# A planner's rules replaced by an order written out by hand, and banks open to all: relu-squared attention and a gated feed-forward layer on one core

## The chip, the cores and the metric

The kernel runs on one NeuronCore of a Trainium2 chip. The metric is device time in microseconds of one execution; the kernel before has a median of 409.42 us over 3 runs. One further execution was recorded by the hardware profiler, and all profile lines come from it.

## The reference

```python
# q, k, v: (8 batches, 12 heads, 448 positions, 64)
scores = (1 / sqrt(64)) * q @ k.transpose
attn   = maximum(scores, 0) ** 2 / 448
x      = (attn @ v), heads side by side           # (3584 tokens, 768)
gate   = maximum(x @ w_gate, 0)                   # w_gate, w_val: 768 x 1536
out    = (gate * (x @ w_val)) @ w_out             # w_out: 1536 x 768, out float32
```

There is no softmax, so a score tile needs only a relu and a square before it is multiplied with V.

## The kernel before

**Engines.** TensorE (PE) does all products and some transposes. VectorE (DVE) and ScalarE (ACT) empty its accumulation banks and do the elementwise work. GpSimd (POOL) issues the loads, SyncE (SP) the transposing transfers and the stores.

**Attention** goes in groups of four heads ("quads"), three to a batch, 24 in all; batch 0 is done in two parts of 192 and 256 query columns, so the list of attention objects `A_` has 27 entries. A group's queries and keys are loaded to `raw`, transposed to `qkT` (for batches 0 and 1 by TensorE, lines L535, L542 and L582; from batch 2 on a copy `perm` on DVE, L606, and then two transposing transfers by SP). `s(step)` (L681) makes one slot of scores: four matmuls on 64x64 tiles of the array, side by side, into a pair of neighbouring banks. Its relu (L692 on ACT or L694 on DVE) and its square (L704 or L706) leave `at`. When all 7 slots of a group are there, `pv()` (L723) multiplies them with V: 28 matmuls on 64x64 tiles into another pair of banks, copied to `xT` (L738 or L740).

**Feed-forward** works on 128x128 tiles. Batches 0 and 1 take plain products (`gv_plain`, L787). The later batches go in pairs through one level of Strassen's method: `gv_strassen` makes seven products (L896) for each of 12 blocks of the hidden width, in three banks, where later products are added to earlier ones after those have been copied out (`snapshot`, L843/L847); `out_both` does the same for the output weights (L1013). So a chain of products keeps a bank for a while.

**Banks.** There are eight. A score slot or a `pv` takes a pair, chosen from PAIRS, MORE_PAIRS or FIRST_PAIRS; a product takes a single one from SINGLES:

```python
    PAIRS, MORE_PAIRS, FIRST_PAIRS = [0, 2], [0, 2, 4], [0, 2, 4, 6]
    SINGLES = [7, 6, 5, 4]
```

**Order.** The program is written as operations (`Op`) with their engines, prices, needed operations and buffers. `plan` walks through planned time: at each step it takes the operation that could start first by the prices, and the emitted program on every engine is the list of operations sorted by planned start. Each engine then runs its own list in that order and waits where an operand or a bank is not ready. Prices are written as (time until the engine is free, time until the result is there), for instance `A448, V448 = (0.455, 0.6), (0.533, 0.66)` for a copy of 448 columns on ACT and DVE. Before, `plan` chooses TensorE's next operation between the head of the attention list (`att`) and a window of the feed-forward list (`ffn`) by a debt account: RESERVE, WINDOW, START, LATEST, HOLD, SLACK, CUTS, SPARE and APART are its settings. The loads form one list for POOL (`pool_ops`), in the order of `Planner.ORDER`; `load_gv` brings two blocks of the gate and value weights, `load_out` a quarter of the output weights. Until 21 us of planned time a `filler` of dummy matmuls (L1169) is put into gaps of TensorE's order.

Of the kernel before, what the change touches and what calls it, by code (L numbers as in the profile page):

```python
# [41 lines left out]
class Op:  # L42


    def __init__(self, engs, emit, deps=(), alloc=(), reads=(), mode=None, grp=None):
        self.engs, self.emit = engs, emit
        self.deps, self.alloc, self.reads = list(deps), list(alloc), list(reads)
        self.mode, self.grp = mode, grp
        self.load = self.land = 0.0
        self.kind = None  # L50
        self.cut = self.edge = False
        self.xbar = 0
        self.start = self.end = self.eng = None
        for b in self.reads:
            b.readers += 1


class Planner:
# [5 lines left out]
    RESERVE = (1000.0, 4.0, 3.0)  # L64
# [4 lines left out]
    WINDOW = (5, 5)  # L69
    ATT_WINDOW = (3, 1)  # L70
    START = (0.7, 0.8)
    LATEST = (1.8, 3.0)
    HOLD = (0.1, 0.05)
    SLACK = (0.2, 0.1)
    CUTS = ((1, 3), (1, 5, 6), (2, 4, 6), (2, 6))
# [7 lines left out]
    SCORES_FIRST = 0.0  # L83
# [4 lines left out]
    SPARE = -0.3  # L88
    APART = (0.5, 0.5)
# [84 lines left out]
def plan(first, att, ffn, others, pool, goals, filler, banks):  # L174

    P = Planner(banks)  # L180
    ai = pi = 0
# [6 lines left out]

    def done(op):
        for o in outs.get(id(op), ()):  # L190
            o.missing -= 1
            if not o.missing:
                active.append(o)

    att, ffn = list(att), list(ffn)
    last_grp = None
    inside, debt, share = False, 0.0, 0.0
    left_work = {}
    for o, sg in ffn:
        left_work[sg] = left_work.get(sg, 0.0) + o.engs["PE"][0]  # L200

    def set_share():
        sg = ffn[0][1] if ffn else None
        left = goals[sg] - ai if sg is not None and goals[sg] is not None else 0
        work = left_work[sg] - P.RESERVE[min(sg, 2)] if left > 0 else 0.0
        return max(0.0, work) / max(1, left)

    def fits(ops, now, late):

        among, width = ops[0].alloc[0].among, ops[0].alloc[0].width  # L210
        times = sorted(max(P.free_at(i + w) for w in range(width)) for i in among)
        for o, t in zip(ops, times):
            if t > now + P.SLACK[late]:
                return False
            now += o.engs["PE"][0]
        return True

    first = [list(x) for x in first]
    while any(first) or att or ffn or active or pi < len(pool):
        cands = []  # L220
        late = int(not ffn or ffn[0][1] >= 3)
        for op in active:
            b = P.best(op)
            if b is not None:
                cands.append((b[0] + P.YIELD.get(op.kind, 0.0), b[2] - P.URGENT.get(op.kind, 0.0), 1, b[1], op, b[0]))
        if pi < len(pool):
            b = P.best(pool[pi])
            if b is not None:
                s = b[0]
                if pi >= P.NOUT:  # L230
                    s = max(s, P.landed[pi - P.NOUT])
                cands.append((s, 0.0, 0, "POOL", pool[pi]))
        pick = None
        if any(first):
            for i, x in enumerate(first):
                b = P.best(x[0]) if x else None
                if b is not None:
                    cands.append((b[0] + (P.SCORES_FIRST if i == 0 else 0.0), b[2], 3, "PE", x[0], b[0]))
            b = P.best(att[0]) if P.SPARE is not None and att else None
            if b is not None:  # L240
                s = b[0] + att[0].engs["PE"][0] + P.SPARE
                if all(c[2] != 3 or s <= c[0] for c in cands):
                    cands.append((b[0], b[2], 4, "PE", att[0]))
        else:
            A = F = None
            for i, op in enumerate(att[:P.ATT_WINDOW[late]]):
                b = P.best(op)
                if b is not None and (A is None or b[0] < A[0] - 0.03):
                    A = (*b, i)
            for i, (op, _) in enumerate(ffn[:P.WINDOW[late]]):  # L250
                b = P.best(op)
                if b is not None and (F is None or b[0] < F[0] - 0.03):
                    F = (*b, i)
            if last_grp is not None and ffn and last_grp == ffn[0][0].grp:
                b = P.best(ffn[0][0])
                F = (*b, 0) if b is not None else None
                pick = "F" if F is not None else None
                if F is not None and A is not None and A[0] + att[A[3]].engs["PE"][0] + P.APART[late] <= F[0]:
                    pick = "A"
            elif A is not None and F is not None:  # L260
                now = P.t.get("PE", 0.0)
                if inside:
                    pick = "A" if A[0] <= max(F[0], now + P.HOLD[late]) else "F"
                else:
                    n = next((i for i, o in enumerate(att) if o.cut), len(att) - 1) + 1
                    if debt >= P.LATEST[late] * n * share:
                        pick = "A" if A[0] <= F[0] + 0.15 else "F"
                    elif debt >= P.START[late] * n * share and A[0] <= now + 0.15 and (ffn[0][0].edge or ffn[0][1] < 3) \
                            and fits(att[:n], now, late):
                        pick = "A"  # L270
                    else:
                        pick = "F" if F[0] <= A[0] + 0.3 else "A"
            elif A is not None:
                pick = "A"
            elif F is not None:
                pick = "F"
            if pick == "A":
                cands.append((A[0], A[2], 2, "PE", att[A[3]]))
            elif pick == "F":
                cands.append((F[0], F[2], 2, "PE", ffn[F[3]][0]))  # L280
        assert cands, f"no operation can start: {ai} {len(ffn)} {len(active)} {pi}"
        c = min(cands, key=lambda c: c[:3])
        s, _, kind, e, op = c[:5]
        if kind in (1, 3):
            s = c[5]
        if e == "PE" and s < P.FILL_UNTIL:
            t0 = max(P.t.get("PE", 0.0), P.FILL_FROM)
# [7 lines left out]
        done(op)  # L295
        if kind == 0:
            pi += 1
        elif kind == 1:
            active.remove(op)
        elif kind == 3:  # L300
            first = [x[1:] if x and x[0] is op else x for x in first]
        elif kind == 4:
            ai += 1
            del att[0]
        elif pick == "A":
            share = set_share()
            debt -= share
            inside = not op.cut
            ai += 1
            i = A[3]  # L310
            if op.cut and i > 0:
                att[i - 1].cut, op.cut, inside = True, False, True
            del att[i]
            last_grp = None
        else:
            sg = ffn[F[3]][1]
            del ffn[F[3]]
            inside = False
            debt += op.engs["PE"][0]
            left_work[sg] -= op.engs["PE"][0]  # L320
            last_grp = op.grp
# [5 lines left out]
def kernel(  # L327
# [77 lines left out]
    A448, V448 = (0.455, 0.6), (0.533, 0.66)  # L405
    A384, V384 = (0.40, 0.54), (0.467, 0.61)
    A896, V896 = (0.83, 0.98), (1.0, 1.13)

    PAIRS, MORE_PAIRS, FIRST_PAIRS = [0, 2], [0, 2, 4], [0, 2, 4, 6]
    SINGLES = [7, 6, 5, 4]  # L410
# [212 lines left out]
    def vec(n, act=True):  # L623

        c = {"DVE": (0.067 + n / 960.0, 0.197 + n / 960.0)}
        if act:
            c["ACT"] = (0.08 + n / 1195.0, 0.23 + n / 1195.0)
        return c

    class Attention:  # L630
# [33 lines left out]
        def s(self, step):  # L664
# [33 lines left out]
            sq = Op({"DVE": (0.07 + c / 960.0, 0.19 + c / 960.0), "ACT": (0.19 + 2 * c / 1195.0, 0.36 + 2 * c / 1195.0)},  # L698
# [161 lines left out]
    def gv_strassen(b, seg, T_ops):  # L860
# [46 lines left out]
        def in_order(mf):  # L907

            start = len(ffn)
# [4 lines left out]
            ffn[start][0].edge = True  # L914

# [104 lines left out]
    def out_both(b, seg, T_ops):  # L1020
# [14 lines left out]
        def in_order(i):  # L1035
            start = len(ffn)
# [7 lines left out]
            ffn[start][0].edge = True  # L1044

# [158 lines left out]
    done_at = {}  # L1204
# [10 lines left out]
    def PV(n):  # L1215
        att.append(A_[n].pv())
        if A_[n].g == NQ - 1:
            done_at[A_[n].b] = len(att)
# [10 lines left out]
    for n in range(NQ, len(A_)):  # L1229
        if n < 2 * NQ:  # L1230
            att.append(late[n - NQ]())
        kind = 0 if n < 2 * NQ else 1 if A_[n].b == 1 else 2 if A_[n].b < Planner.MORE_UNTIL else 3
        for i in range(len(A_[n].steps)):
# [6 lines left out]
            if i in Planner.CUTS[kind]:  # L1240
                att[-1].cut = True
        if n in (2 * NQ - 1, len(A_) - 1):
            PV(n)
        if n == 2 * NQ - 1:
            part_two = len(att)
    goals = [part_two, done_at[1]]
# [6 lines left out]
    for p in range(B // 2):  # L1253
# [3 lines left out]
        goals.append(done_at.get(2 * p + 3))  # L1257

    for op in plan(first, att, ffn, others, pool_ops, goals, filler, r_ps):
# [31 lines left out]
```

## Time and profile before

| what | value |
|---|---|
| runs | 409.42 us median, 408.06 lowest, 411.56 highest, 3 runs |
| profiled execution, first to last instruction (span) | 407.7 us |
| TensorE matmuls | 397.1 us busy, 3460 instructions |
| VectorE | 324.9 us busy, 570 instructions |
| ScalarE | 263.0 us busy, 395 instructions |
| GpSimd | 75.6 us busy |
| mean granted TensorE clock | 0.990 |
| reads and writes of HBM | 47.19 and 11.01 MB |

The page gives no time of the profiled execution beside its span; the runs, timed without the profiler, are 0.4 to 3.9 us above it. An engine's busy time counts its instructions from start to end; for TensorE, whose matmuls overlap in a pipeline, it also covers the small gaps between them. The sum of a stage therefore has to be taken from start to start.

### The profile page before, as it was taken

The numbers are of one execution on the slowest core, as the hardware profiler recorded it, in microseconds if no ns is written. First come the engines' busy times: TensorE is split into PE (matmuls) and PEld (weight loads), VectorE is DVE, ScalarE is ACT, GpSimd is POOL, SyncE is SP. The second block draws the span as 40 slices with busy tenths as digits, with TensorE's granted clock in tenths as the row PEclk, the third lists the DMA queues.
The fourth block names the chain that finished last, engine by engine and source line by source line (L and its number), as shares of the span: only waits on it lengthen the run. The fifth ranks groups of instructions, "written<-read, shape, count | busy, mean of one in ns | idle before, by whom it ended". The sixth has DMA issues, their size and how long they took to land.

```text
span 407.7 us, 8763 instructions
## 1 busy us (share of the span) xinstructions
PE 397.1 (97%) x3460; PEld 207.2 (51%) x3460; DVE 324.9 (80%) x570; ACT 263.0 (65%) x395; POOL 75.6 (19%) x121
## 2 busy tenths in 40 slices
PE   8789999999999999999999999999999999999995
PEld 4587744444445544444454544444445555555663
DVE  4988674998688798999897998898799657677652
ACT  3878873896686886878587887476686544343221
POOL 7856142122211222102122112110000000000000
PEclk9969999999999999999999999999999999999999
DMA  9999999998779997688878999542002430000244
GB/s 116 187 197 199 200 131 169 159 150 102 92 110 183 142 182 99 74 99 113 82 102 143 168 176 170 76 50 36 2 1 55 100 80 0 2 0 2 72 113 127
DMA packets 77305, 43.44 MB, mean 107 GB/s; under 512 B 40912, under 2 KB 77264, under 8 KB 77264
## 3 DMA queue, kind: packets, MB, share of 16 engines
q0 software_dynamic: 34896, 23.60, 44.0%
q1 hardware_dynamic: 42048, 18.89, 28.3%
q8 instruction: 27, 0.44, 0.4%
q10 hardware_dynamic: 320, 0.39, 0.3%
q14 instruction: 14, 0.11, 0.1%
HBM read 47.19 MB, written 11.01 MB: 143 GB/s over the span
## 4 chain that ended last, share of the span: by engine, by line
PE 91%; DMA 3%; DVE 3%; ACT 2%; issue 0%; ACTq 0%; SPq 0%; DVEq 0%
PE ps L896 36%; PE ps L1013 24%; PE ps L787 12%; PE ps L681 9%; PE ps L723 8%; DMA qkT<-perm 3%; PE ps L1169 2%; ACT at L692 2%; DVE at L694 1%; PE ps L535 1%; PE ps L582 1%; DVE at L706 1%; DVE xT L740 0%; DVE o L1003 0%; DVE hT L938 0%
## 5 line engine op out<-in xcount | busy, mean ns | idle before, releaser
L692 ACT ACTIVATE at<-ps 128x896 bf16<-128x896 f32 (+4 forms) x109 | 94.8, 907 | 17.1 <-PE ps L681 17.0
L843 ACT COPY f<-ps 128x448 f32<-128x448 f32 x100 | 52.8, 531 | 55.3 <-PE ps L896 52.0
L694 DVE TENSOR_SCALAR at<-ps 128x896 bf16<-128x896 f32 (+4 forms) x62 | 66.4, 1073 | 9.5 <-PE ps L681 6.5
L704 ACT ACTIVATE at<-at 128x896 bf16<-128x896 bf16 (+3 forms) x71 | 65.3, 937 | 2.1 <-DVE at L694 1.6
L706 DVE TENSOR_TENSOR at<-at 128x896 bf16<-128x896 bf16 (+3 forms) x100 | 59.0, 613 | 1.1 <-ACT at L692 0.9
L681 PE MATMUL ps<-qkT 64*64 64x448 bf16 (+2 forms) x756 | 51.8, 349 | 3.0 <-DMA qkT<-perm 1.0
L896 PE MATMUL ps<-xT,gvT 128*128 128x448 bf16 x216 | 52.8, 353 | 0.0
L896 PE MATMUL ps<-sx,wv 128*128 128x448 bf16 x216 | 52.2, 353 | 0.0
L896 PE MATMUL ps<-xT,wg 128*128 128x448 bf16 x216 | 51.7, 353 | 0.2 <-DVE at L694 0.2
L896 PEld LDWEIGHTS <-gvT 128*128 128x128 bf16 x324 | 30.0, 98 | 32.6 <-issue 6.9
L1013 PEld LDWEIGHTS <-sh 128*128 128x128 bf16 x312 | 29.2, 98 | 23.7 <-issue 4.2
L422 POOL DMA_DIRECT2D raw<-in_k_dram x18 | 11.3, 628 | 138.9 <-DVE perm L606 113.5
L723 PE MATMUL ps<-at,vv 64*64 64x448 bf16 (+2 forms) x700 | 34.7, 335 | 1.2 <-ACT at L704 0.8
L422 POOL DMA_DIRECT2D vv<-in_v_dram x44 | 26.6, 616 | 49.0 <-PE ps L681 46.4
L1013 PEld LDWEIGHTS <-hT 128*128 128x128 bf16 x270 | 25.5, 98 | 19.9 <-issue 3.6
L1013 PE MATMUL ps<-wo,hT 128*128 128x384 bf16 x192 | 35.5, 327 | 0.0
L681 PEld LDWEIGHTS <-qkT 64*64 64x64 bf16 x756 | 18.9, 109 | 29.3 <-issue 24.5
L845 ACT ACTIVATE f<-ps 128x384 f32<-128x384 f32 x37 | 18.1, 490 | 23.9 <-PE ps L1013 21.0
L787 PE MATMUL ps<-xT,wg 128*128 128x448 bf16 (+2 forms) x180 | 32.7, 319 | 0.3 <-DVE at L694 0.3
L938 DVE TENSOR_TENSOR hT<-ps,g 128x448 bf16<-128x448 f32 x36 | 22.4, 622 | 13.1 <-PE ps L896 12.9
L787 PE MATMUL ps<-xT,wv 128*128 128x448 bf16 (+2 forms) x180 | 32.2, 315 | 0.0
L1003 DVE SCALAR_TENSOR_TENSOR o<-ps,f 128x384 f32<-128x384 f32 x41 | 22.7, 554 | 11.0 <-PE ps L1013 10.2
(70 smaller groups left out, 496.8 us busy)
## 6 DMA issues: line engine op xcount, KB each, us to landing
out_dram<-o SPq DMA_DIRECT2D x108, 96.0 KB, 2.2
vv<-in_v_dram POOLq DMA_DIRECT2D x44, 112.0 KB, 6.9
raw<-in_k_dram POOLq DMA_DIRECT2D x18, 224.0 KB, 4.8
raw<-in_q_dram POOLq DMA_DIRECT2D x18, 224.0 KB, 7.0
wo<-in_moe_w_out_dram POOLq DMA_DIRECT2D x4, 576.0 KB, 12.0
wg<-in_moe_w_gate_dram POOLq DMA_DIRECT2D x5, 384.0 KB, 9.3
wv<-in_moe_w_val_dram POOLq DMA_DIRECT2D x5, 384.0 KB, 10.4
gvT<-in_k_dram POOLq DMA_DIRECT2D x6, 224.0 KB, 6.9
```

Source lines behind the costliest of these rows:

```text
L422: op = Op({"POOL": (0.5 + 0.0004 * n_desc,) * 2}, lambda: nc.gpsimd.dma_start(out=dst(), in_=src), deps=deps, alloc=alloc)
L681: nc.tensor.matmul(banks()[64 * j:64 * j + 64, z, h2], lhsT=self.k_of(j, h2, k), rhs=self.q_of(j, h2), start=True, stop=True)
L692: nc.scalar.activation(self.at_of(i, m), banks(), AF.Relu)
L694: nc.vector.tensor_scalar_max(self.at_of(i, m), banks(), 0.0)
L704: nc.scalar.activation(a, a, AF.Square)
L706: nc.vector.tensor_tensor(a, a, a, ALU.mult)
L723: nc.tensor.matmul(ps[64 * h2:64 * h2 + 64, ps2.idx + j, :n], lhsT=st.v_of(j, h2, c), rhs=self.at_of(c)[64 * j:64 * j + 64, 0, h2], start= ...
L787: nc.tensor.matmul(ps[:, pb.idx, z * n:(z + 1) * n], lhsT=w[:, kd, fc], rhs=xT_t[xbuf[b].idx][:, kd, cols], start=(kd == 0), stop=(kd == K ...
L843: nc.scalar.copy(dst, src)
L896: nc.tensor.matmul(ps[:, pb.idx, :S], lhsT=w(g)[:, fc], rhs=rhs, start=start and g == 0, stop=stop and g == KH - 1, skip_group_check=True)
L1003: op = Op({"DVE": V384}, lambda: nc.vector.scalar_tensor_tensor(o_t[ob.idx], ps[:, pb.idx, :OH], float(out_scale), f_t[fb.idx][:, :OH], AL ...
L1013: nc.tensor.matmul(ps[:, pb.idx, :OH], lhsT=lhs(kf), rhs=rhs(kf), start=start and kf == 0, stop=kf == FH - 1, skip_group_check=True)
```

## The change

The settings of the debt account go away, with the code that used them. In their place stand three strings. PE_ORDER names TensorE's operations one by one: a small letter takes the operation at that place (a is the first) of what is left of the attention list, a capital one of what is left of the feed-forward list. LOAD_ORDER does the same for the loads. AHEAD shifts the planned start at which each operation of the other engines competes, by a tenth of a microsecond for each letter from m. The planner still walks through time, but TensorE's and POOL's order are now given. PAIRS, MORE_PAIRS and SINGLES name all banks, some prices are changed, and a filler starts no earlier than the end of the memset of its operand.

```diff
+PE_ORDER = (
+    'aacddcaddbaadacehbeadabbafecaadbDGaCADAcabaAAicadcbGGaaaHAGFadbcdbGcaAKcaEIaeaaECFGcaaGHGAADcCBAFEMNNdfeBAGbaa'
+    'CAAaeFEADeabaaLAIJFFAbaDAgbbdaACcaaEAAcefAAaBaAbaaAAAccbAdaaBCBAaaABcAAAacBBabAcbaAAABcGAEAADABBAGJCDAEABBBBAB'
+    'aeDAaaADDCBAcBAABbaACAAacbcaDAGJACCBEACAACACAdcCBBaaEBAEACabacaCBBEBBBABaaDBBACAAbaacaAACFABgbFECEAbaBEAeabdCb'
+    'bAefaBCECAecdABaaaAAAAaaacBAADaaDBDACAAEBCAcbDAHBAGAABAAAacAGAAaabBAAAAAABAAAbbaCAAIAAAbbaDAADbcCBAAGAdaAGaaGAB'
+    'ACDABaaedBCDCCDAADABdaBACAAAafaFAGBaaaAAdaAbaIBAaaaBACdcACbaAAAaBCABABABABBAAABAAAAAABAAAAAABAAAAAABAAAAAABAAA'
+    'AAABAAAAAABAAAAAABAAAAAABAAAAAABAAAAAABABABDAAAAAAAAACBBAAAAAAABABBBA'
+)
+LOAD_ORDER = (
+    'aaaaaaaaaaaaaaaaaaaaaaaaaaaaaaaaaaaaaaaaaaaaaaabcbaaaaaaaaacccaaaaabaaaaaaaaaaaaaaaaaaaaaaaaaaaaaaaaaaaaaaaaaa'
+    'aaaaaaa'
+)
+AHEAD = (
+    'mknnnllkmkkmlkkkmnolnlonnonlkmnnoknmmmmmlmnmlnmnnnmknnkolomlonkmklomllllkmmmkokkmjknmlllnkjolknmlpolokkpnlklln'
...
+def arranged(ops, letters, base):
+
+    left, out = list(ops), []
+    for c in letters:
+        out.append(left.pop(ord(c) - ord(base)))
+    return out + left
...
+    lines = {'a': sum(first, []) + list(att), 'A': [o for o, _ in ffn]}
+    pe = []
+    for c in PE_ORDER:
+        base = 'a' if c.islower() else 'A'
+        pe.append(lines[base].pop(ord(c) - ord(base)))
+    pe += lines['a'] + lines['A']
+    pool = arranged(pool, LOAD_ORDER, 'a')
+    for o in others:
+        o.wait = P.YIELD.get(o.kind, 0.0)
+    for o, c in zip(others, AHEAD):
+        o.wait = round(o.wait + (ord(c) - ord('m')) * 0.1, 3)
...
-                cands.append((b[0] + P.YIELD.get(op.kind, 0.0), b[2] - P.URGENT.get(op.kind, 0.0), 1, b[1], op, b[0]))
+                cands.append((b[0] + op.wait, b[2] - P.URGENT.get(op.kind, 0.0), 1, b[1], op, b[0]))
...
+        if ai < len(pe):
+            b = P.best(pe[ai])
             if b is not None:
...
+                cands.append((b[0], b[2], 2, "PE", pe[ai], b[0]))
...
-            t0 = max(P.t.get("PE", 0.0), P.FILL_FROM)
+            t0 = max(P.t.get("PE", 0.0), P.FILL_FROM, still.end or s)
...
-    A448, V448 = (0.455, 0.6), (0.533, 0.66)
-    A384, V384 = (0.40, 0.54), (0.467, 0.61)
+    A448, V448 = (0.43, 0.585), (0.535, 0.665)
+    A384, V384 = (0.375, 0.54), (0.469, 0.605)
...
-    PAIRS, MORE_PAIRS, FIRST_PAIRS = [0, 2], [0, 2, 4], [0, 2, 4, 6]
-    SINGLES = [7, 6, 5, 4]
+    PAIRS, MORE_PAIRS, FIRST_PAIRS = [0, 2, 4, 6], [0, 2, 4, 6], [0, 2, 4, 6]
+    SINGLES = [7, 6, 5, 4, 3, 2, 1, 0]
...
-            c["ACT"] = (0.08 + n / 1195.0, 0.23 + n / 1195.0)
+            c["ACT"] = (0.055 + n / 1200.0, 0.225 + n / 1200.0)
...
-            sq = Op({"DVE": (0.07 + c / 960.0, 0.19 + c / 960.0), "ACT": (0.19 + 2 * c / 1195.0, 0.36 + 2 * c / 1195.0)},
+            sq = Op({"DVE": (0.07 + c / 960.0, 0.19 + c / 960.0), "ACT": (0.105 + 2 * c / 1200.0, 0.27 + 2 * c / 1200.0)},
```

## The prediction

> **What bounds the kernel now.** I read the page first, then TensorE's own waits, the chain of waits, TensorE's timeline around 157 us and at the start, and the table of stretches for the other engines.
>
> ```profile
> span 407.7 us, 8763 instructions
> ...
> PE 397.1 (97%) x3460; PEld 207.2 (51%) x3460; DVE 324.9 (80%) x570; ACT 263.0 (65%) x395; POOL 75.6 (19%) x121
> ...
> PE 91%; DMA 3%; DVE 3%; ACT 2%; issue 0%; ACTq 0%; SPq 0%; DVEq 0%
> ```
>
> TensorE is busy for 97% of the span, and the chain that ended last runs through it for 91%. The question is whether it also waits. Its waits between 27 and 403 us are these, all of them:
>
> ```profile
> PE ps L681 <- DMA qkT<-perm: 1.0, 1, 1.0
> PE ps L787 <- DVE at L694: 0.3, 1, 0.3
> PE ps L896 <- DVE at L694: 0.2, 1, 0.2
> ```
>
> So after the first 27 us only a cheaper TensorE stream can shorten the kernel: three waits, 1.5 us, are all that a better placing could win. What the stream costs beyond its work is seen where it goes from 64x64 tiles (L681 scores, L723 products with V) to 128x128 tiles (L787, L896, L1013) and back. From the chain of waits:
>
> ```profile
> 110.95 0.69 PE ps L681 x12
> ...
> 157.46 0.50 PE ps L681 x8
> 157.96 1.24 PE ps L896 x6
> 159.20 1.45 PE ps L723 x28
> ...
> 182.70 0.67 PE ps L896 x3
> ```
>
> Twelve score matmuls take 0.69, eight 0.50: four matmuls, one slot, are 0.19, and 0.13 of a run is fixed. Six products take 1.24, three 0.67: three are 0.57, and 0.10 is fixed. Each 64x64 run with the 128x128 run behind it thus pays about 0.235 us for changing over, whatever its length. (The busy figure hides this, since it counts the change as busy.)
>
> **The start** is not bound by TensorE's work alone:
>
> ```profile
> 16.00:20.00 4.00, 2.61 (x89) 2.09 (x92) 4.00 (x7) 4.00 (x9) 3.42 (x6) 1.00 1.48 181
> 20.00:24.00 4.00, 3.15 (x77) 2.84 (x72) 3.76 (x7) 3.04 (x6) 1.23 (x2) 0.58 1.63 189
> 24.00:28.00 4.00, 3.74 (x61) 3.37 (x52) 3.15 (x5) 2.96 (x5) 2.21 (x4) 0.56 1.28 202
> 28.00:32.00 4.00, 4.00 (x89) 3.75 (x90) 3.72 (x8) 2.93 (x6) 3.15 (x6) 1.00 1.33 199
> ```
>
> ```profile
> 24.41 2.24 PE L681 MATMUL ps<-qkT 64*64 64x256 bf16 x36
> 26.91 0.93 PE L787 MATMUL ps<-xT,wg 128*128 128x192 bf16 x6 [0.26 <-DVE at L694]
> ...
> 30.24 0.97 PE L582 MATMUL ps<-ident,gvT 128*64 128x128 bf16 x28
> ```
>
> The granted clock (column before the last two) is 0.58 and 0.56 from 20 to 28 us and 1.00 afterwards; the trace's clock record has one stretch of 0.5 from 20.7 to 27.5. The transposes of batch 1's first quad (L582, call it T3) start at 30.24, and from there TensorE is never short of work for long.
>
> **The change part by part.**
>
> *The order of TensorE.* I replayed PE_ORDER against the two lists it picks from (208 attention operations, 411 feed-forward operations; a small letter takes that place of the first list, a capital of the second). It uses up both lists exactly. The work is the same; the grouping is not. From T3 on the trace of before has 85 runs of 64x64 tiles and 86 of 128x128; the letters give 64 and 65. In before 16 of the 85 are a single score slot, with the letters 3.
>
> The sum for before, from T3 on, by the rows above: 147 score slots at 0.187 give 27.4; V products (1.45 less the fixed 0.13) 29.2; transposes 2.7; plain feed-forward 51.6; Strassen products (L896) 142.9; output products (L1013) 96.4: work 350.2. Change-overs 85 x 0.13 + 86 x 0.105 = 20.1. Sum 370.3. Measured: 402.33 (last matmul's result taken by DVE) less 30.24 is 372.1. The sum leaves 1.8 us of waits, near the 1.5 that the view of waits names; so the prices hold.
>
> With the letters: one V product of 256 columns (0.75) has moved ahead of T3, work 349.5; change-overs 64 x 0.13 + 65 x 0.105 = 15.1. Sum 364.6, which is **5.7 us less**. All of it lies on the path: no other engine covers a change-over.
>
> *When T3 starts.* The first 47 loads keep their order, and the queue of GpSimd is paced by them; in the trace batch 1's first keys and queries (issued at 16.95 and 17.58) landed at 26.17 and 27.55. T3 cannot start before **27.6**. Ahead of it the letters put the value product of block 3, whose weights landed at 22.85, with four more products, three score steps and a V product behind it: 4.2 us with that one at full clock, to 27.1, so that the load decides and T3 starts at 27.6. With half clock until 27.5, 2.3 of the 4.2 are done by then and T3 starts at 29.4; with half clock all the way, 31.3. In before the score steps stood ahead of the feed-forward products and T3 came at 30.24. I take **28.9**, nearer to the half-clock case, because the letters still leave TensorE waiting for that weight, and the clock had fallen in before after 4 us with 2.6 busy (16 to 20). Bounds 27.6 and 31.3.
>
> The Trainium skill ("TensorE: Matmul & The Clock Gate", sections "HAM oscillation — how this bites in real kernels" and "A second HAM failure mode: psum-queue depth-cycling") holds that the clock halves after a window of about 3.4 us with TensorE idle, and that cycling through PSUM banks with small gaps can bring the same; the second speaks against letting every tile use any bank. The row says less of the first (the clock fell though TensorE was about 65% busy) and nothing for the second (1.00 from 28 us to the end while banks rotate all the time). By the skill's rule alone T3 would be at 27.6 and the forecast 1.3 us lower; each later window at half clock, as an estimate from that page, would add 1.7.
>
> *Any bank.* PAIRS and SINGLES only widen choice, no instruction is added. The most that it can win after T3 is the 0.5 us in the two waits of L787 and L896 for an `at` evacuation; it may lose, since products can now sit in banks that a score pair needs whole. That is the slower rival below.
>
> *Priorities and the new cost figures.* Counts on DVE and ScalarE stay (a relu or copy may change engine). The planner's prices come down to what the trace shows back to back: ScalarE relu of 896 elements 0.83 to 0.80 (shortest start to start 0.797), square 0.94 to 0.85 (0.840), 448-column copy 0.455 to 0.43 (0.428). So ScalarE is given more, which it has room for:
>
> ```profile
> 27.00:100.00 73.00, 71.99 (x772) 41.22 (x772) 58.62 (x89) 55.51 (x83) 24.14 (x36) 1.00 1.24 161
> 100.00:200.00 100.00, 99.67 (x804) 46.94 (x802) 87.97 (x155) 73.49 (x106) 18.29 (x30) 1.00 0.85 119
> 200.00:322.00 122.00, 122.00 (x997) 59.67 (x995) 108.05 (x193) 86.96 (x125) 13.40 (x22) 1.00 0.58 90
> ```
>
> DVE is busy 80 to 89% and ScalarE 71 to 76% in the three stretches with attention. Squeezing 285 us of it by 2% leaves both below TensorE. I cost this at nothing; the cover is that idle 11 to 29%, and where it is missing in a burst TensorE waits, which is the next term.
>
> *Waits of TensorE after T3.* The fixed order waits at its head and lets nothing pass. Two places look tight. The letters of the loads put an output weight (576 KB) ahead of the value weights of blocks 10 and 11 (they landed at 67.39) on GpSimd's queue, behind the raw load that waits for the `perm` copy; about 3 us more, at some 155 GB/s, makes 70.4, and the letters reach that product at 68.6 if T3 is at 28.9. Batch 2's third quad is reached at 94.5, and its transposing DMA landed at 94.11, the one that cost 1.0 before. Elsewhere the distance from the last score step of a group to its V product is 2.2 us or more of TensorE's time; a DVE relu (1.07) and a square (0.61 DVE, 0.95 ScalarE) fit with 0.2 to spare. Lower bound 0.5 (every wait placed away but one of those), upper bound the slower rival's; I take **3.0**, the 1.8 of before and 1.2 for the loads. Fillers now begin no earlier than their operand's memset; they began behind it anyway (1.39), so nothing.
>
> *The end.* Last matmul to the end of the span: 407.7 - 402.33 = **5.4**. ScalarE stood 3.7 us for an output buffer and evacuated the last tile only at 403.60; without that 1.2 less, with one more store in front as much more. I keep it.
>
> **The sum:** 28.9 + 364.6 + 3.0 + 5.4 = 401.9 us of span against 407.7. The median of the runs, 409.42, is 1.7 above that span (lowest 408.06, highest 411.56); carried over, 403.6.
>
> **Rivals.**
> (a) *The start wins everything.* T3 at 27.6, waits 1.0, tail 4.9: 398.1, as a run 399.8. For: the products are moved ahead of the last score steps. Against: the weights' landing.
> (b) *Waits eat it.* A searched order leaves no slack, and every late evacuation or load shows. Before's order stalled 1.8; 8.5 in its place gives 407.4, as a run 409.1. For: the two loads above, the 0.2 to spare. Against: the old plan, whose prices were coarser, came out with 1.8.
> (c) *Slower: pairs of banks.* From T3 on 11 runs need four or five bank pairs one after the other (two scores, V product, scores); before had 4. With two chains of feed-forward products open and a bank or two not yet evacuated, two pairs are left, and the V product waits for the first relu: 0.2 to stream, 0.2 until its end (one matmul lasts 0.35), 0.9 to evacuate, 1.3 us a run, 11 x 1.3 = 14.3. That gives 416.2, as a run 417.9. It decides from 0.9 a run on (413.5). For: five of the 11 runs start with one or two chains open. Against: none starts with more, which leaves three pairs if they lie well; the V product's own 1.3 us is time to evacuate; and before's run of that kind at 228.2 took 2.23 for 2.05 of streaming, no wait.
> That the change does nothing is out: the run counts differ.
>
> **How the numbers follow.** Forecast 0.58, (a) 0.13, (b) 0.23, (c) 0.06. One per cent, about what a measurement of this kernel can tell from no change, is 4.1 us: faster is below 405.3, slower above 413.5. The forecast and (a) give faster 0.70 (a sliver of the forecast's chance lies above); (b) gives same, with that sliver, 0.24; (c) slower 0.06. The range reaches from (a), 0.9 further down for a tail without the buffer wait, to just past (b): 398.9 to 409.5.
>
> **What would show it.** Right: about 65 runs of each kind after T3; fixed parts still 0.13 and 0.10; T3 between 27.6 and 29.5; TensorE's waits after it near 3 us, at the weights of block 10 or at qkT. Wrong: many waits of L681 or L723 for `at` evacuations (b, c), a second stretch of half clock, or T3 no earlier than 30.

## Result and profile after

| | before | after |
|---|---|---|
| median of 20 runs each, us | 408.34 | 407.25 |
| lowest and highest run, us | 407.21, 411.56 | 405.06, 409.84 |
| time of the profiled execution, its span, us | 409.42, 407.7 | 405.06, 403.3 |

The ratio after to before is 0.9961, 95% interval 0.9942 to 0.998. (Ratios, here and below, leave out the few runs that took over 1.5% more than the fastest of the same kernel; medians are of all runs.) The kernel is faster by about 0.4%. The time lies inside the range that was forecast, but the move is little more than a quarter of the 1.4% forecast. By the forecast's bound of one per cent this is no change.

The page of after first: span, busy times, shares of the chain that ended last.

```profile
span 403.3 us, 8702 instructions
...
PE 390.1 (97%) x3452; PEld 209.1 (52%) x3452; DVE 323.6 (80%) x568; ACT 267.6 (66%) x397; POOL 75.6 (19%) x121
...
PE 88%; DMA 6%; ACT 2%; DVE 2%; issue 1%; SPq 0%; DVEq 0%
```

TensorE's busy time fell by 7.0 us at the same products; some 2.3 of it are the fillers, which take 4.9 us in the timeline of after and 7.2 in that of before. The chain that ended last now runs through transfers for 6% of the span, against 3%. These are all of TensorE's waits between 30 and 400 us (line, what it waited for, then us in total, times, longest):

```profile
PE ps L613 <- DMA qkT<-perm: 1.4, 1, 1.4
PE ps L719 <- DMA wv<-in_moe_w_val_dram: 0.9, 1, 0.9
PE ps L514 <- ACT at L624: 0.2, 1, 0.2
PE ps L613 <- ACT qkT L440: 0.2, 1, 0.2
```

2.7 us, of which 2.2 are at two transfers: the value weights that the prediction named, and a `qkT` transfer, of another quad than the one it named (L613 is now the scores, L719 the plain products, L514 the transposes of T3). The price of a change-over, from the chain of waits of after (L655 is the product with V, L828 Strassen):

```profile
156.16 0.50 PE ps L613 x8
156.67 1.24 PE ps L828 x6
...
161.92 0.32 PE ps L613 x4
...
167.99 1.32 PE ps L655 x28
169.32 0.38 PE ps L613 x8
```

Four scores are 0.18 here, and 0.14 of a run is fixed (0.13 before); six products are 1.24 as before. Scores that follow a V product pay no fixed part (0.38 for eight). The two prices stand, and only the number of change-overs fell: from T3 on the trace has 64 runs on 64x64 tiles and 65 on 128x128, as many as the prediction counted from the letters.

The other engines in the three stretches of attention:

```profile
27.00:100.00 73.00, 70.34 (x751) 40.93 (x753) 57.70 (x87) 53.00 (x78) 22.87 (x33) 1.00 1.18 157
100.00:200.00 100.00, 100.00 (x838) 49.74 (x827) 88.78 (x155) 74.69 (x109) 17.73 (x30) 1.00 0.84 116
200.00:322.00 122.00, 122.00 (x1016) 61.98 (x1017) 109.94 (x196) 94.20 (x133) 15.74 (x26) 1.00 0.62 101
```

DVE (the third pair) is busy 79 to 90%, ScalarE (the fourth) 73 to 77%. The start is where it went the other way:

```profile
8.00:12.00 4.00, 3.23 (x90) 2.12 (x84) 3.01 (x7) 3.43 (x7) 2.81 (x5) 1.00 1.36 185
12.00:16.00 4.00, 3.55 (x97) 2.85 (x92) 3.48 (x9) 3.64 (x6) 3.47 (x5) 0.77 1.32 183
16.00:20.00 4.00, 3.33 (x74) 2.78 (x69) 2.65 (x6) 3.01 (x5) 3.83 (x6) 0.50 1.46 165
20.00:24.00 4.00, 3.40 (x112) 2.60 (x109) 3.34 (x7) 3.70 (x7) 1.25 (x3) 0.87 1.63 190
```

The granted clock falls at 14.2 us, 6.5 us earlier than in the profile of before, and is back at 21.0. T3 starts at 30.04:

```profile
30.04 0.97 PE L514 MATMUL ps<-ident,gvT 128*64 128x128 bf16 x28
```

### The profile page after: what moved, and what is told of

It reads as the page before. It is cut to its first block, busy times and chain, and to the rows that moved or that the text cites. A ratio compares the mean times of both kernels' runs of the same rounds, so it can differ in the third digit from the quotient of the medians.

```text
span 403.3 us, 8702 instructions
## 1 busy us (share of the span) xinstructions
PE 390.1 (97%) x3452; PEld 209.1 (52%) x3452; DVE 323.6 (80%) x568; ACT 267.6 (66%) x397; POOL 75.6 (19%) x121
## 3 DMA queue, kind: packets, MB, share of 16 engines
q1 hardware_dynamic: 42048, 18.89, 27.5%
## 4 chain that ended last, share of the span: by engine, by line
PE 88%; DMA 6%; ACT 2%; DVE 2%; issue 1%; SPq 0%; DVEq 0%
PE ps L828 36%; PE ps L943 25%; PE ps L613 10%; PE ps L719 9%; PE ps L655 7%; DMA qkT<-perm 6%; ACT at L624 1%; PE ps L1097 1%; DVE at L626 1%; ACT qkT L440 0%; PE ps L514 0%; SPq L544 0%; DVE at L638 0%; ACT xT L670 0%; PE ps L467 0%
## 5 line engine op out<-in xcount | busy, mean ns | idle before, releaser
L624 ACT ACTIVATE at<-ps 128x896 bf16<-128x896 f32 (+4 forms) x116 | 101.8, 908 | 28.1 <-PE ps L613 26.9
L636 ACT ACTIVATE at<-at 128x896 bf16<-128x896 bf16 (+1 forms) x72 | 67.1, 949 | 2.8 <-DVE at L626 2.2
L626 DVE TENSOR_SCALAR at<-ps 128x896 bf16<-128x896 f32 (+3 forms) x55 | 58.5, 1065 | 7.0 <-PE ps L613 6.2
L613 PE MATMUL ps<-qkT 64*64 64x448 bf16 (+2 forms) x756 | 51.4, 347 | 4.3 <-DMA qkT<-perm 1.4
L828 PE MATMUL ps<-sx,wv 128*128 128x448 bf16 x216 | 51.7, 353 | 0.0
L828 PE MATMUL ps<-xT,gvT 128*128 128x448 bf16 x216 | 51.6, 353 | 0.0
L828 PE MATMUL ps<-xT,wg 128*128 128x448 bf16 x216 | 50.6, 353 | 0.0
L828 PEld LDWEIGHTS <-gvT 128*128 128x128 bf16 x324 | 31.1, 98 | 30.3 <-issue 2.0
L943 PEld LDWEIGHTS <-sh 128*128 128x128 bf16 x312 | 29.7, 98 | 22.4 <-issue 3.0
L655 PE MATMUL ps<-at,vv 64*64 64x448 bf16 (+2 forms) x700 | 34.9, 337 | 0.0
L613 PEld LDWEIGHTS <-qkT 64*64 64x64 bf16 x756 | 19.3, 108 | 29.3 <-issue 21.8
L777 ACT ACTIVATE f<-ps 128x384 f32<-128x384 f32 x39 | 19.2, 492 | 21.6 <-PE ps L943 20.5
L719 PE MATMUL ps<-xT,wv 128*128 128x448 bf16 (+2 forms) x180 | 31.0, 316 | 0.9 <-DMA wv<-in_moe_w_val_dram 0.9
L894 DVE CUSTOM_DVE_ANT_0 g<-ps,f 128x448 bf16<-128x448 f32 x36 | 22.3, 621 | 11.5 <-PE ps L828 7.3
L828 PEld LDWEIGHTS <-wv 128*128 128x128 bf16 x216 | 20.4, 98 | 21.3 <-issue 3.4
L828 PEld LDWEIGHTS <-wg 128*128 128x128 bf16 x216 | 20.5, 98 | 20.6 <-issue 2.4
```

What stands on the lines that cost most here:

```text
L613: nc.tensor.matmul(banks()[64 * j:64 * j + 64, z, h2], lhsT=self.k_of(j, h2, k), rhs=self.q_of(j, h2), start=True, stop=True)
L624: nc.scalar.activation(self.at_of(i, m), banks(), AF.Relu)
L626: nc.vector.tensor_scalar_max(self.at_of(i, m), banks(), 0.0)
L636: nc.scalar.activation(a, a, AF.Square)
L655: nc.tensor.matmul(ps[64 * h2:64 * h2 + 64, ps2.idx + j, :n], lhsT=st.v_of(j, h2, c), rhs=self.at_of(c)[64 * j:64 * j + 64, 0, h2], start= ...
L719: nc.tensor.matmul(ps[:, pb.idx, z * n:(z + 1) * n], lhsT=w[:, kd, fc], rhs=xT_t[xbuf[b].idx][:, kd, cols], start=(kd == 0), stop=(kd == K ...
```

## Experiments

All kernels were profiled, and timed against the kernel before on the same chip. Theories: **A**, the order does what the sum says after T3, and the start gives it back; **B**, the searched order leaves waits after T3 that eat the gain; the experiments' own texts say what each means in the run at hand.

### Both kernels once more

The same two programs, unchanged; a single profile of each was all that the prediction and the first comparison had.

> The changed kernel once more, unchanged. Its 20 runs had spans from 403.3 to 408.0 us, and the mean granted clock goes with them: at 0.996 to 1.000 they lie between 403.3 and 405.1, at 0.987 to 0.991 between 405.9 and 408.0. Theory A (the start decides: after the change TensorE is warmed later and less, so more of the start runs at half clock) expects the same split here, ratio 0.994 to 0.998, and in a second profile a T3 that moves with the half-clock stretch while the part after T3 stays within 1 us of 373.3. Theory B (the fixed order waits for late transfers after T3, by a different amount each time) expects T3 near 30 again and the spread after it.

> The kernel before once more, unchanged, for the granted clock of each of its runs and a second profile. Theory A expects a mean clock of 0.994 or more in most runs and spans of 405.5 to 408 with T3 at 28.5 to 30.5; if the clock is as low as in the changed kernel's runs (0.987 to 0.992 in half of them), the start is no worse after the change and theory A falls. Theory B expects no difference in clock, and 372 to 373 us from T3's start to the last matmul in every profile.

After: 0.9957 (0.9937 to 0.9976), 406.92 us. Before: 0.9995 (0.9958 to 1.0033), 408.55 us. The profiles differ from the first ones. Before now has its first scores at 6.73 instead of 7.80, no half clock in the start, and T3 at 28.39 instead of 30.24. After has half clock twice in its start (from 16.3 and 23.2, 3.4 us each) and T3 at 31.22. TensorE's only wait of before between 27 and 400 us was

```profile
PE ps L896 <- DVE at L694: 0.2, 1, 0.2
```

so the profile that the prediction was built on showed a slower start of before than this one, and the first profile of after one of its faster executions (405.06 is the lowest of its 20 runs).

### The start: fillers and their operand

After, the first filler starts at 3.31; in the profiles of before it was 1.39. DVE and TensorE at the start, from the timeline of after:

```profile
0.83 0.17 DVE L1074 MEMSET ident<- 128x128 bf16 x1 [0.83 <-PEq L1193]
...
2.82 0.43 DVE L1084 MEMSET woT<- 128x448 bf16 x1
```

```profile
3.31 4.05 PE L1097 MATMUL ps<-woT 128*128 128x421 bf16 x11 [3.31 <-DVE woT L1084]
7.28 0.91 PE L467 MATMUL ps<-ident,gvT 128*64 128x128 bf16 x28
8.23 0.41 PE L613 MATMUL ps<-qkT 64*64 64x192 bf16 x8
```

The second letter of AHEAD puts the building of the identity ahead of the fillers' memset, and the block of fillers runs on to 7.3. The experiment moves the memset back to the front:

```diff
-    'mknnnllkmkk...
+    'mnnnnllkmkk...
```

> The changed kernel with one letter of AHEAD changed, so that DVE writes the operand of the dummy matmuls before it makes the identity, as in the kernel before: the dummy matmuls then begin near 1.4 us and no longer at 3.3. Nothing else moves but their number. Theory A expects a higher mean clock and 1 to 2.5 us less than the changed kernel (ratio to the kernel before 0.990 to 0.994). Theory B expects no difference (0.995 to 0.998).

0.9967 (0.9944 to 0.999), 406.74 us: nothing won. The first scores did come at 6.86, but half clock followed from 15.3 to 22.1, and T3 was at 29.93. So putting the filler early does not by itself bring the start back.

The plan shows a second thing. `filler` may use banks 6 and 7 alone (`pb = bank([6, 7])`), and with all banks open to scores and products these two are taken: the plan places fillers at 1.8, 7.4 and 17.5 us, and leaves out those that would fit at 9.5, 12.4 and 14.6. The next kernel has the edit above and fillers in any bank (it also lets them go on to 33 us, but its trace shows none that starts behind 18.1):

```diff
-    FILL_UNTIL = 21.0
+    FILL_UNTIL = 33.0
...
-        pb = bank([6, 7])
+        pb = bank(None)
```

> The changed kernel with the memset first (as in fill_first) and dummy matmuls allowed in any bank and until 33 us of planned time: three more gaps of the planned start (0.9, 0.6 and 0.8 us, at 9.5, 12.4 and 14.6) are filled, which the kernel before had filled too while banks 6 and 7 were left to them. Theory A (the start, by the clock) expects a mean clock of 0.995 or more in most runs, T3 at 28 to 29 in place of 29.9 to 31.2, and 1.5 to 2.5 us less than the changed kernel: ratio 0.989 to 0.993. If T3 is set by the loads and by DVE and ScalarE alone, the clock rises and the time does not: 0.995 to 0.997. Theory B (waits after T3) expects 0.995 to 0.997 too.

The text says that the kernel before had filled these gaps too. It had not filled the last two: its trace has fillers at 8.2, 8.8, 10.5 and 18.4 us and none between 10.5 and 18.4. So the edit does more than give back what the change had taken.

0.9898 (0.9847 to 0.9949), 403.49 us. First scores at 7.10, T3 at 27.61, no half clock until the end of the span. The stretches of this kernel:

```profile
12.00:16.00 4.00, 3.84 (x104) 2.71 (x103) 3.34 (x8) 3.72 (x7) 3.95 (x5) 1.00 1.33 175
16.00:20.00 4.00, 3.23 (x121) 2.54 (x114) 3.76 (x9) 3.82 (x5) 3.44 (x6) 1.00 1.50 173
20.00:24.00 4.00, 3.67 (x104) 2.79 (x97) 3.94 (x7) 4.00 (x7) 1.24 (x2) 1.00 1.63 190
```

Against the same rows of after, what has changed is the clock, and with it DVE and ScalarE, which are fed again (3.76 and 3.82 of 4 us against 2.65 and 3.01 at 16 to 20). Run a second time on another chip:

> The same as warm, for a narrower interval (it was 0.985 to 0.995). Theory A: ratio near 0.990, T3 at 27.6 to 28.2, and the wait for the second quad's transposing transfer near 78 to 80 us again 1.5 to 3.5.

0.9879 (0.9846 to 0.9911), 403.71 us, T3 at 28.03. To tell the two edits apart, the bank edit alone and once more both, side by side:

```diff
-        pb = bank([6, 7])
+        pb = bank(None)
```

> The new kernel with one edit: a filler may sit in any free bank instead of banks 6 and 7. The identity stays ahead of the memset, so the first filler still starts at about 3.3. By the plan this adds fillers at 9.5, 12.4 and 14.6 us and nothing else. Theory A (the open banks took the fillers' banks, and the empty gaps cost the start): this edit alone gives most of what the two edits together gave, 0.988 to 0.992 of before (404 to 405.5 us), T3 at 28.0 to 29.0 because the first scores are still 0.6 late, and no stretch at half clock before 28 us. Theory B (both edits are needed: the late first filler costs as much): 0.993 to 0.997, T3 at 29 or later.

> The kernel with both edits once more (the later end of the fillers adds none in its plan), beside the one-edit kernel on the same chip. Theory A: within 0.3% of the one-edit kernel, 0.987 to 0.991 of before. Theory B: 0.987 to 0.991 too, and 0.5% or more faster than the one-edit kernel. T3 at 27.6 to 28.1 in both.

The bank edit alone: 0.9909 (0.9875 to 0.9944), 405.24 us. Both: 0.984 (0.9799 to 0.9882), 403.88 us on the same chip. Neither theory's numbers fit all of it. The bank edit alone gives the ratio that A named and no half clock in the start. The medians of the two are 0.34% apart and the ratios 0.7%, with intervals that overlap, where A allowed 0.3%; the times alone don't settle whether the early memset adds anything. But T3 of the bank edit alone is at 29.46, later than A allowed:

```profile
8.39 0.51 PE L613 MATMUL ps<-qkT 64*64 64x192 bf16 x8
...
29.46 0.97 PE L514 MATMUL ps<-ident,gvT 128*64 128x128 bf16 x28
```

With both edits these are at 6.94 and 28.01: the 1.45 us at the first scores arrive whole at T3. One profile of each is little, since the block of early fillers itself took 4.25 to 5.43 us from profile to profile; over the five profiles that have both edits T3 is at 28.03 in the mean (27.61 to 28.35), again 1.4 us ahead. Put beside `fill_first`: the early memset brought its gain only where the clock held. The starts together (first scores, half clock ahead of T3, T3, and the time between the first and the last of these, us):

| kernel | first scores | half clock | T3 | between |
|---|---|---|---|---|
| before | 7.80 | 20.7 to 27.5 | 30.24 | 22.4 |
| before_again | 6.73 | none | 28.39 | 21.7 |
| before_few (below) | 6.74 | none | 28.10 | 21.4 |
| after | 8.23 | 14.2 to 21.0 | 30.04 | 21.8 |
| after_again | 7.66 | two of 3.4 | 31.22 | 23.6 |
| fill_first | 6.86 | 15.3 to 22.1 | 29.93 | 23.1 |
| old_loads (below) | 8.39 | none | 29.64 | 21.3 |
| any_bank | 8.39 | none | 29.46 | 21.1 |
| warm, warm_2, warm_3 | 7.10, 6.59, 6.94 | none | 27.61, 28.03, 28.01 | 20.5, 21.4, 21.1 |
| warm_old_loads, two_perm (below; both filler edits) | 7.86, 7.61 | none | 28.13, 28.35 | 20.3, 20.7 |

Without half clock the time from first scores to T3 is 20.3 to 21.7 in either order, with it 21.8 to 23.6. T3 is the one plus the other.

One profile shows one execution, but every timed run has its mean granted clock on record, and a run with as much half clock as the profile of after has 0.992 or less. With the new order and fillers in banks 6 and 7 (`after`, `after_again`, `fill_first`, `old_loads`) 36 of 56 runs are that low; with fillers in any bank (`any_bank` and the three of `warm`) none of 27; with before's order 2 of 12 in `before_again`, 1 of 12 in `before_few`, and 11 of the 79 runs of before that were timed beside the others. (In `warm_old_loads` and `two_perm`, which have the filler edits and more, 5 of 15 are; there half clock can lie in mid kernel, as the last section tells.) Within one program it shows in the time: the runs of after at 0.992 or less have a median of 408.27, those at 0.996 or more 406.24; in after_again 407.52 and 406.63.

Whether fillers as such decide was tried on the kernel before, which lost all of them behind 7 us:

```diff
-    FILL_UNTIL = 21.0
+    FILL_UNTIL = 7.0
```

> The kernel before with the dummy matmuls after 7 us left out (three gaps, 1 us in all). Theory A expects the clock of its runs to fall from 0.993 to 1.000 to what the changed kernel shows (0.987 to 0.996), T3 to come 1 to 2 us later and the ratio to be 1.002 to 1.005. If the dummy matmuls of that stretch don't matter, 0.999 to 1.001 with the clock as before.

1.0003 (0.998 to 1.0026), 408.89 us, T3 at 28.10, no half clock in the start. A's expectation failed: before's own order does not need these fillers. That filling the gaps holds the clock is shown for the new order alone.

### The loads

The output weight that LOAD_ORDER pulls forward goes back behind the value weights of blocks 10 and 11 (one letter group of LOAD_ORDER, `bcb`, becomes `aaa`), first in after, then with both filler edits:

> The changed kernel with the output weight back behind the weights of blocks 10 and 11 and behind batch 2's second quad on GpSimd's queue, as before. Theory B expects the wait for those weights (0.4 to 0.9) to go and the wait for the transposing transfer near 80 us (1.4 to 2.4) to shrink by about 1: ratio 0.992 to 0.995. If the second wait is TensorE simply arriving earlier at a transfer that lands near 80 us anyway, only the first goes and the second grows by as much: 0.995 to 0.997. Theory A expects no change, 0.995 to 0.997.

> Both edits. If the start and the loads each cost what theories A and B say, the gains add: 0.986 to 0.991. If the transfer near 80 us is a floor, an earlier T3 is given back there in a longer wait and the ratio stays within 0.002 of old_loads alone.

0.9973 (0.9948 to 0.9998), 407.76 us, and 0.9896 (0.9845 to 0.9948), 406.1 us as the median of six runs that reach from 401.51 to 408.84: against the same kernels with the new loads no difference that can be told. The waits tell why. After's 0.9 at `wv` is gone in `old_loads`, and in its view of waits between 30 and 400 us

```profile
PE ps L613 <- DMA qkT<-perm: 2.4, 1, 2.4
```

stands where after had 1.4: the second wait took what the first gave up. This wait is for the second quad of batch 2: its transposing transfer landed at 80.76 in after, 80.44 in the first profile of before, 78.22 in before_again, and whoever comes earlier waits. With T3 at 27.61, the timeline of warm shows

```profile
75.81 0.38 PE L613 MATMUL ps<-qkT 64*64 64x448 bf16 x4
77.99 0.38 PE L613 MATMUL ps<-qkT 64*64 64x448 bf16 x4 [1.80 <-DMA qkT<-perm]
```

The last experiment on this moves that transfer: the first two copies to `perm` of batch 2 are planned 3 us earlier, and the second goes to free space in `woT`, so that it need not wait for the first transfer to have read `perm`; both on top of the filler edits.

```diff
+    for o in [o for o in others if o.kind == "perm"][:2]:
+        for x in [o] + outs[id(o)]:
+            x.start -= 3.0
...
+    def perm_of(b, g):
+        if (b, g) != (2, 1):
+            return perm_t[0]
+        flat = woT.rearrange("p a f m -> p (a f m)")[:, 512:512 + 4 * NT * D]
```

> The kernel of warm, with the perm copies of batch 2's first two quads moved 3 us earlier in DVE's order and the second of them put into a second place (a part of woT that is free until 88 us), so that it no longer waits for the first quad's transposing transfer to land (63.2). If the wait near 78 us is TensorE arriving at a transfer that stands behind that chain (copy, transfer, copy, transfer), the second transfer lands 2 to 4 us earlier, the wait falls under 0.5 and the ratio is 0.003 to 0.006 below warm's. If the transfer is held by the share of the DMA engines that the loads take, it lands within 1 us of before and the ratio is warm's.

0.9912 (0.9875 to 0.9949), 406.09 us. The transfer landed at 75.93, and its timeline has the eight scores without a wait:

```profile
78.16 0.57 PE L622 MATMUL ps<-qkT 64*64 64x448 bf16 x8
```

The time is no better than that of warm. T3 to the last matmul takes 368.35, no less than warm's 367.93, because other waits stand where that one stood (0.87 at 33.8, 0.59 at the value weight at 70.4, 0.72 at 227.0): 2.6 us in all, against 2.3 in warm. Why these came is not settled. Three of its nine runs also have a granted clock of 0.992 or less, and took 407.5 to 407.8.

### The strings one by one

Three kernels keep the open banks and the new prices and take strings away. `order_only`: AHEAD and LOAD_ORDER empty. `old_order`: the same, and PE_ORDER names the order that before had. `old_start`: all strings, but PE_ORDER with before's order up to T3.

```diff
 PE_ORDER = (
-    'aacddcaddbaadacehbeadabbafecaadbDGaCADAcabaAAicadcb...
+    'aaccccaaaajaaagacadaabbbaabccaaabccAAAAAABAaaicadcb...
```

> The changed kernel with PE_ORDER alone: AHEAD and LOAD_ORDER empty, so that the other engines and the loads go by the planner's own rules. If the letters for TensorE carry the change and the others are trimming, 0.995 to 1.002. If the three strings hold each other up (a fixed order of TensorE that waits wherever another engine comes in another order), 1.01 to 1.03, with waits of 5 us and more for evacuations after T3.

> The changed kernel with the TensorE order of the kernel before written as letters, AHEAD and LOAD_ORDER empty: only the open banks and the new prices differ from the kernel before. If open banks and prices alone cost or win nothing, 0.998 to 1.003 and 85 runs of 64x64 tiles after T3. If they shift the other engines against an order made for other banks, 1.005 to 1.03 with new waits after T3.

> The changed kernel with TensorE's order of the kernel before up to T3, and the new letters' order for all that is left. Theory A expects the gain of the change-overs to show: ratio 0.987 to 0.992. Theory B expects no more than the changed kernel has (0.994 to 1.0). It has the shifts of AHEAD that were found for another start, which may cost it up to 2 us in either theory.

`order_only`: 1.0103 (1.0055 to 1.015), 412.49 us. T3 at 29.12, but T3 to the last matmul is 376.5, with TensorE's waits between 30 and 400 us

```profile
PE ps L648 <- ACT at L617: 2.0, 2, 1.0
PE ps L606 <- ACT xT L663: 1.9, 2, 1.0
PE ps L606 <- DMA qkT<-perm: 1.2, 1, 1.2
PE ps L606 <- ACT at L617: 1.1, 1, 1.1
```

mostly for evacuations on ScalarE that stand too late in its list (L606 and L648 are scores and V products here). The view counts 6.7 us of waits in all. Without them this stage still takes 369.8, against after's 365.8; by the starts of the matmuls most of the rest lies between one score and the next, in pauses too short for the view. `old_order`: 1.0159 (1.0114 to 1.0204), 415.1 us, T3 to the last matmul 383.3, with a wait of 3.39 for DVE at 309.9, one of 2.26 for `qkT`, and 10.2 us at half clock (from 83.2 and 308.5). `old_start`: 1.0256 (1.0225 to 1.0287), 419.55 us; the shifts of AHEAD were made for another order of TensorE, and the new waits (4.26 for values at 116.2 the longest) hide what the start did. Its output is not the reference's either, for a reason that no run here shows. This one says nothing of the start.

In a row: old order under the open banks 1.016, its letters 1.010, AHEAD and the loads 0.996, the fillers 0.984 to 0.990. The order of TensorE alone doesn't beat before; with the planner's plain rules for DVE, ScalarE and the loads it loses. Not run: the letters with before's sets of banks, for which no plan exists, so the price of the open banks alone is open.

## Why the prediction was right about the change-overs and wrong about the start

I take the two profiles of after and the three of before's order (the third with fewer fillers in the start), mean of each, and the start of the last matmul as the end of the stage, which is 0.6 us later than the point the prediction used (402.95 against 402.33 before; at 402.33 DVE took an earlier result, not that of the last matmul).

| term, us | before | after | difference | predicted |
|---|---|---|---|---|
| T3 | 28.9 | 30.6 | +1.7 | -1.3 |
| T3 to last matmul, without waits | 371.5 | 365.9 | -5.6 | -5.7 |
| waits of TensorE in it | 1.0 | 3.1 | +2.1 | +1.2 |
| behind | 4.8 | 4.8 | 0 | 0 |
| sum | 406.2 | 404.4 | -1.8 | -5.8 |

**The change-overs: right.** 5.7 us were forecast and 5.6 found, with fixed parts and counts as forecast. 5.0 of the forecast are change-overs; the other 0.7 is a V product that moved ahead of T3 and is paid there. Nor is it luck: without waits this stage takes 371.4 to 371.6 in the three profiles of before's order, and 365.7 to 366.3 in all seven of the new order with its shifts that have no half clock behind T3. **The waits: right** in size, and half right in place: 3.0 forecast, 2.7 and 3.4 measured, at the value weight and at `qkT`. What was a little off is the 1.8 for before: it read 1.5 from the view and has 1.0 over three profiles. The landing of the `qkT` transfer was named for the third quad of batch 2; it was the second. **The end and the other engines: right** for this kernel: TensorE waits only 0.2 us at a time for them. But the cover was costed at nothing because of its idle share, and `order_only` shows that the share does not do it: the same TensorE order, without the shifts of AHEAD and the new order of loads, waits 6.7 us, 5.0 of it for ScalarE. It is the place in the list that hides the work; idle time alone does not.

**When T3 starts: wrong, and this is the step that failed.** Forecast 28.9, bounds 27.6 to 31.3; found 30.0 and 31.2. A gain of 1.3 us was forecast and a loss of 1.7 found: 3.0 of the 4.0 us by which the sum was off. Two of the prediction's own signs of being wrong came: T3 no earlier than 30, and in after_again a second stretch of half clock. Three things were missed in it.

First, before's T3 of 30.24, from which the gain of 1.3 was reckoned, was that of one execution with half clock and late first scores (7.80); two others have 28.1 and 28.4. The text knew that half clock had cost that execution and still let it stand as the base. For the same reason carrying the difference of one execution over to the median was unsafe: the profiles of before span 405.0 to 407.7, more than the effect, and the 409.42 that the forecast was set against, the median of three runs, lies 1.1 above the median of twenty.

Second, "they began behind it anyway (1.39), so nothing". The rule about the memset does cost nothing; what makes the first filler late is the memset's own place, which AHEAD moves behind the identity. The text counted AHEAD as work for DVE and ScalarE and did not ask which operations of DVE something early waits for. Measured: first filler 3.31 instead of 1.39, first scores at 7.66 to 8.39 in the five profiles with the late memset and 6.59 to 7.86 in the eleven with the early one, and 1.4 us of T3 where the clock held (`any_bank`, one profile, against the five with both edits).

Third, "PAIRS and SINGLES only widen choice, no instruction is added". The text weighed bank pairs after T3 and overlooked that banks 6 and 7 belonged in part to the fillers. With the banks open the plan leaves three gaps empty that fillers would fit. Giving fillers any bank brought 0.9909 against 0.9957 and 0.9961, 0.5%, and no half clock ahead of T3 in any of the six profiles with that edit; of the four profiles of the new order without it, three have half clock. The granted clocks of the timed runs agree (36 of 56 low without the edit, none of 27 with it and nothing else but the early memset). So the empty gaps cost the new order its clock. That the clock is the whole way by which they cost time is not shown: fewer waits of DVE and ScalarE go with it. It is no rule either, since before's order kept its clock without its later fillers in 11 of 12 runs (`before_few`).

The Trainium skill ("TensorE: Matmul & The Clock Gate", section "HAM oscillation — how this bites in real kernels") ties half clock to waits of more than about 3.4 us. In after the longest idle stretch of TensorE between the first scores and 14.2 was 0.73 us, so here the row decides: the clock also fell on a TensorE with many short gaps. The page's section "A second HAM failure mode: psum-queue depth-cycling" does tell of a clock that goes up and down with frequent short pauses, in a kernel that cycles through banks. The pauses are seen in this start, but the open banks as such did not bring it here: after has 1.00 from 21.0 to its last matmul, with every bank open all the while.

**The rivals.** (a), the start wins all, is near what the two filler edits make of the kernel: T3 at 27.6 to 28.0 in the three profiles of warm, 0.2 to 0.6 us behind the landing of the queries (27.4 in each), and 403.5 to 403.9 us. It did not come to (a)'s 399.8. One reason is that the waits did not shrink to 1.0: the earlier TensorE meets the same `qkT` transfer and waits 1.8 to 2.3; another is half clock in mid kernel, told below. (b) gives a time near the result, but not by its way: the waits are 3, not 8.5. (c), bank pairs, is refuted for this kernel: no V product waited for a pair after T3. In `order_only`, with the same banks and the same order of TensorE, two did wait 1.0 each for a relu on ScalarE, the kind of wait that (c) describes; so it is the shifts of AHEAD (or the order of the loads), not the letters, that keep it away.

**The best version** is the new kernel with both filler edits, by ratio 0.984 to 0.990 of before and by medians 0.987 to 0.988, about 403.7 us.

## What to carry to other kernels

Counting changes of tile shape and pricing them from pairs of rows in one trace gave what TensorE's own stream saved to 0.1 us, but a saving on the busiest engine ends at the next transfer that does not move with it, and at whatever was taken to pay for it. When a resource is opened to all, list who had it for himself before, the dummy work too; when a list of shifts is added, look first at the handful of early operations that something waits for. And take several profiles before a forecast of one per cent: the start of one program varied by 1.9 us from one profile to the next here.

## What was not expected of the hardware

Ahead of the last matmul, half clock came in stretches of 3.4 us or its multiples in every profile (3.4, 6.8, 10.2 in the clock records), and not in every execution of a program. The kernel before had 2.61 of 4 us busy at 16 to 20 in one profile and half clock from 20.7, while before_again kept full clock with no more work:

```profile
16.00:20.00 4.00, 2.54 (x88) 1.91 (x85) 4.00 (x8) 4.00 (x8) 3.29 (x6) 1.00 1.51 185
20.00:24.00 4.00, 2.99 (x88) 2.23 (x88) 3.56 (x7) 3.26 (x6) 1.25 (x3) 1.00 1.63 189
```

What decides between the two is open; whether it matters what TensorE does while it is busy (transposes, products) was not tried. A single wait in mid kernel can go with it too. In warm_2, warm_3 and warm_old_loads the waits of 2.3, 2.2 and 3.6 us at `qkT`, which ended at 79.0, 79.5 and 80.1, were joined by half clock from 79.4, 80.3 and 78.9, for 3.4, 3.4 and 6.8 us. In six other profiles of the new order the wait at the same place (1.4 to 2.4 us) had none. So a wait of this size costs itself and sometimes more: without its waits the time from T3 to the last matmul is 367.6 in warm_2 and in warm_3 and 368.5 in warm_old_loads, against 365.9 in the mean of the seven without half clock there, which makes 1.7 us for a stretch of 3.4 and 2.6 for one of 6.8. That the wait brings the half clock, and not only goes with it, is not shown.
